# Attention and two gated layers in one kernel: scores merged in PSUM, six low weight halves formed by TensorE and ScalarE, and a new order of steps

## The chip, the cores and the metric

One core of a Trainium2 chip runs the whole program. Its engines are TensorE (PE; its weight loads stand in rows of their own, PEld), VectorE (DVE), ScalarE (ACT), GpSimd (POOL) and SyncE (SP), whose queue issues all DMAs here. The metric is the time of one execution on the device in microseconds, and of several executions the median.

## The reference

Three stages follow one another. Sliding-window attention over 4 batches, 8 heads, 576 positions and head size 64; a feed-forward layer with layer norm on 512 columns and 2048 hidden ones; and a gated layer with GELU, a second layer norm and a product over the sequence.

```python
scores = scale * np.matmul(q, k.transpose(0, 1, 3, 2))
mask = (rel >= 0) & (rel < window)                    # window = 128, rel = row - column
scores = np.where(mask, scores + bias[None], -1e9)    # bias = -slope(head) * |rel|
attn = softmax(scores); x = attn @ v
...
xn = (x - mu) / np.sqrt(var + 1e-06) * g_ln           # x: 4 x 576 x 512
x = x + np.maximum(xn @ w_ch1, 0.0) @ w_ch2           # 512 x 2048, 2048 x 512
...
u, v = split(gelu(x @ w_in))                          # 512 x 1024
v_s = np.einsum('ts,bsd->btd', w_sg, layernorm(v) * g_ln) + b_sg
x = x + (u * v_s) @ w_out
```

The weights come as float64 numbers.

## The kernel before

Phase 1 does attention and the feed-forward layer together, phase 2 the gated layer.

Attention is cut into runs (two query tiles of 128 rows for a pair of heads of a batch; at the end of the sequence a tail) and each run into units, one for each query tile: 72 units, numbered `un`. A query tile of 128 rows sees its own key tile (the columns up to its row) and the previous one (the columns after its row), so that each row needs exactly 128 scores, taken from two tiles. `scores` (L436) writes both tiles' scores of a run into PSUM. `unit` then copies the previous tile's scores to an SBUF tile `t` (L451, ACT or DVE, as the planner chooses; for the first tile of a sequence POOL fills `t` with a large negative number, L467), writes the own tile's scores over it under a mask (L480, `copy_predicated`), adds the distance bias and takes the row's minimum (L486), does the exponentials on ACT (L490), sums and inverts (L493, L494), normalises (L498 on POOL, or L451 on ACT through the same helper), transposes on PE (L508) and writes the two triangles to the tiles `m` (L522 on DVE, or L525 on ACT with L445 on POOL). `values` (L575) multiplies with v, and L555 copies the result to `x`.

The feed-forward layer runs over nine groups `g` of 256 rows. `norm`, `center`, `rest` and `spread` do the layer norm: mean products (L597), `xc` (L610), `xh` (L623), `xl` (L629), squares (L639), their products (L654), the power on POOL (L660) and the spread of rstd (L664). `m1` (L738) and `m2` (L749) are the two products of a step. Every fp32 product is made of three fp32r products of a high and a low half, which is why each operand exists as `h` and `l`. `relu` gives `hh` (L677, ACT) and `hl` (L679, DVE).

Weights are loaded in 40 pieces (`weights(n)`; n below 24 are three quarters of w1 and w2 in pieces of 512 columns; n = 0 to 3 are w1 of the first quarter and 4 to 7 its w2). A piece arrives as float64 and is turned to float32 by the steps of `Split64`: the absolute value of the high word on ACT (L71), and on DVE a clamp (L77), a shift (L79) and two merging steps (L81, L84). Then ACT rounds to the high half (L348), and POOL or DVE subtracts for the low half (L351, "lo"). Phase 2 uses the same steps for its weights (`split64`, L88 and L89 the last two).

The order on every engine's queue is set ahead of time by `Sched`: each task is a generator of `Op`s with an engine, an assumed duration, a priority, the tokens it needs and the buffers it takes. It places, again and again, the ready step with the smallest (start time, priority, number). Constants steer it: HOP and HOPD (time from a step's end to its reader), DVEX (a charge that DVE must undercut where a step could go to another engine), PACE (the priority of units over their number), WFIRST and WBACK (how far ahead of need the weights are put), LQ, OB, OC (offsets in the layer norm, at the transposes and at the values). Unit priorities are the values of PACE; the layer norm of group 0 has start[0] - 14 plus LQ. The first MoE products need the weights 0 to 3 and the four `xl` of group 0, whose input is the values of runs 0 to 3 (units 0 to 7).

```python
# in Split64.bits, the view that steps 0 and 1 (L77, L79) work on, in place
y, yi = (z.rearrange("p (a b) -> p b a", b=2) for z in (x, xi))
# in warm: a product without a reader, when PE has nothing else, until weights piece 23 is done (L790)
yield Op("PE", 110, 10 ** 9)
```

Of the kernel before, what the change touches and what calls it, by code (L numbers as in the profile page):

```python
# [7 lines left out]
F32 = mybir.dt.float32  # L8
F32R = mybir.dt.float32r
U8 = mybir.dt.uint8  # L10
I32 = mybir.dt.int32
ACTF = mybir.ActivationFunctionType
ALU = mybir.AluOpType
# [8 lines left out]
NEG = -1.0e30  # L22
FMAX = float(np.finfo(np.float32).max)
# [11 lines left out]

HOP, HOPD = 160, 127
MOE = 1365
DVEX = 300


PACE = [(0, -61), (7, -47), (8, -46), (15, -32), (16, 4), (23, 12)]
EARLY = 28
WBACK, WFIRST = 5, 40
LBACK = 14, 26
OB, OC = 2, 4
LQ = 0, 1, 2, 3, 4, 8
EPRI = (-1, 9)
# [8 lines left out]
ABANK = 1, 3, 5  # L56


class Split64:


# [11 lines left out]
    def bits(self, k):  # L73
        dve, x, xi = self.nc.vector, self.x, self.x.bitcast(I32)
        y, yi = (z.rearrange("p (a b) -> p b a", b=2) for z in (x, xi))
        if k == 0:
            dve.tensor_scalar(y, y, E_MIN, E_MAX, ALU.max, ALU.min)  # L77
        elif k == 1:
            dve.tensor_scalar(yi, yi, 3, 0x3FFFFFFF, ALU.logical_shift_left, ALU.bitwise_and)  # L79
        elif k == 2:  # L80
            dve.scalar_tensor_tensor(out=xi, in0=self.wh, scalar=-0x40000000, in1=xi, op0=ALU.bitwise_and,  # L81
                                     op1=ALU.bitwise_or)
        else:
            dve.scalar_tensor_tensor(out=xi, in0=self.wl, scalar=29, in1=xi, op0=ALU.logical_shift_right,  # L84
                                     op1=ALU.bitwise_or)
# [28 lines left out]
class Sched:  # L114
# [40 lines left out]
    def run(self, until):  # L155
        while until not in self.done:
            best = None
            for n, p in enumerate(self.procs):
                t = self.ready(p)
# [21 lines left out]
            if op.size:  # L181
                self.dma = max(self.dma, start + 1100) + op.size / 360
                end = self.dma + 1600
            elif op.eng:
                end += HOPD if op.eng == "DVE" else HOP
            if op.token:
# [31 lines left out]
def phase1(tc, nc, a, x2d, cst, p2):  # L218

    sync, act, dve, pool, pe = nc.sync, nc.scalar, nc.vector, nc.gpsimd, nc.tensor  # L220
    ident, ones, g1, mh = cst
    sched = Sched()
# [18 lines left out]
    dist = ap2.tile([128, 12, 128], BF16, name="dist", bufs=1)  # L241
    mask, munf = (ap2.tile([128, 2, 128], U8, name=z, bufs=1) for z in ("mask", "munf"))
    sms = [ap2.tile([128, 8], F32, name="sm%d" % z, bufs=1) for z in range(3)]
# [80 lines left out]
    def weights(n):  # L324
# [12 lines left out]
        j.first()  # L337
        yield Op("DVE", 10 + 1.05 * w, pri)
        j.bits(0)
        yield Op("DVE", 10 + 1.05 * w, pri)  # L340
        j.bits(1)
# [5 lines left out]
        h, l = ((w1 if z < 4 else w2)[q][y][:, z % 4, c] for y in range(2))  # L347
        act.activation(out=h, in_=j.x, func=ACTF.Copy)  # L348
        o = Op(None, 0, pri, token=("w", n), alt=[("POOL", 150 + 2.15 * w, 0), ("DVE", 64 + 1.05 * w, DVEX, 1)])
        yield o  # L350
# [106 lines left out]
    def unit(e):  # L457
# [3 lines left out]
        pri = e.tau  # L461
        sl = [("t", 4, ("T", un))]
        to = [("t", un - 1)] if un else []
        if i == 0:
            yield Op("POOL", 250, pri, need=to, slots=sl, token=("t", un))
            t = ap2.tile([128, 2, 128], F32, tag="t", name="t", bufs=4)
            pool.memset(t, NEG)  # L467
            yield Op(None, 0, pri, need=[("A1", n)])
        else:
            o = Op(None, 0, pri, need=to + [("A1", n)], slots=sl, token=("t", un),  # L470
                   alt=[("ACT", 360), ("DVE", 395, DVEX)] if n in ABANK else [("ACT", 270), ("DVE", 335, DVEX)])
            yield o
            t = ap2.tile([128, 2, 128], F32, tag="t", name="t", bufs=4)
            for h, x in s.parts:
                scaled(o.eng, t[:, h], x[..., u, 0:128])
        w = 64 if tail else 128
        yield Op("DVE", 395 if n in ABANK else 335, pri, need=["msk"], token=("cp", n) if e.last else None)
        for h, x in s.parts:
            k = mask[:, tail, 0:w] if isinstance(h, int) else mask[:, tail:tail + 1, 0:w].to_broadcast([128, 2, w])
            dve.copy_predicated(t[:, h, 0:w], k, x[..., u, 128:128 + w])  # L480
        yield Op("DVE", 425, pri, need=["al2" if tail else "al"], port=True, slots=[("sm", 3, ("nm", un))])
        st = sms[un % 3]
        sums = st[:, 2:6].rearrange("p (h z) -> p h z", h=2)
        for h in range(2):
            d = 8 + s.p + h if tail else 2 * s.p + h
            dve.tensor_tensor_reduce(out=t[:, h], in0=t[:, h], in1=dist[:, d], scale=-0.125, scalar=FMAX, op0=ALU.add,  # L486
                                     op1=ALU.min, accum_out=st[:, h:h + 1])
        yield Op("ACT", 775, pri)
        for h in range(2):
            act.activation(out=t[:, h], in_=t[:, h], func=ACTF.Exp, bias=st[:, h:h + 1], scale=-1.0,  # L490
                           accum_out=sums[:, h, 0:1])
        yield Op("DVE", 160, pri)
        dve.tensor_reduce(out=st[:, 6:8], in_=sums, axis=AX.X, op=ALU.add)  # L493
# [259 lines left out]
    def constants():  # L753
# [6 lines left out]
        sched.free["DVE"] = 2300  # L760
        yield Op("DVE", 200, -1000, need=["cst0"], token="msk")
        dve.tensor_copy(mask, t[:, 3:5])
        yield Op("ACT", 300, -1000, need=["cst0"], token="cst")
        act.activation(out=ident, in_=t[:, 0], func=ACTF.Copy)
        for x0 in range(0, 8, 2):
            yield Op("DVE", 270, -1000, need=["cst0"], token="al" if x0 == 6 else None)
            for x in (x0, x0 + 1):
                dve.tensor_scalar(dist[:, x], t[:, 1], 2.0 ** (2 - x), None, ALU.mult)
# [10 lines left out]
    def warm():  # L779

        z = np_.tile([128, 256], F32, tag="rstd", name="zero", bufs=3).bitcast(BF16)
        dve.memset(z, 0.0)
        ps = ps_a.tile([128, 2, 256], F32, tag="a0", name="warm").rearrange("p a b -> p (a b)")
        for n in range(NWARM):
            pe.matmul(ps, z[:, 0:128], z, start=True, stop=True)
        sched.free["PE"] = 4000
        yield Op(None, 0, 0, need=["al"])
        while ("w", 23) not in sched.done:
            yield Op("PE", 110, 10 ** 9)
            pe.matmul(ob[:, 256:512], dist[:, 0], dist[:, 0:2], start=True, stop=True, skip_group_check=True)  # L790
            yield Op(None, FILL, 10 ** 9)
# [380 lines left out]
def body(tc, nc, a):  # L1172
# [3 lines left out]
    with tc.manual_schedule(), tc.tile_pool(name="cst", bufs=1) as cp:  # L1176
        ident = cp.tile([128, 128], F32, name="ident")
        ones = cp.tile([128, 128], F32, name="ones")
        g1 = cp.tile([128, 4], F32, name="g1")
        mh = cp.tile([128, 1], F32, name="mh")  # L1180
        pool.memset(mh, -0.5)
        pool.memset(ones, 1.0 / DM)
        p2 = Phase2(tc, nc, a, x2d, mh)
        phase1(tc, nc, a, x2d, (ident, ones, g1, mh), p2)

# [47 lines left out]
```

## Time and profile before

| | |
|---|---|
| time, median of 3 runs | 777.67 us (775.90 to 778.61) |
| the profiled execution | 777.32 us, of which the span is 775.2 us |
| PE busy | 749.7 us (97%) |
| DVE busy | 476.5 us (61%) |
| ACT busy | 321.2 us (41%) |
| POOL busy | 217.4 us (28%) |
| mean granted clock of TensorE | 0.976 of full speed |

Matmuls are pipelined, and one of 256 fp32r columns has a row of 0.28 us though the next starts 0.11 us later; so PE counts as busy also where rows only overlap. A row with "x8" joins neighbouring instructions of one kind. Behind a row, square brackets give the idle time of the engine ahead of it and what ended it. On DVE the next instruction often starts some 0.08 us before the row of the last one ends.

### The profile page before, as it was taken

What the parts mean: (1) busy time and instruction counts of PE and PEld (TensorE: products, weight loads), DVE (VectorE), ACT (ScalarE), POOL (GpSimd) and SP (SyncE); (2) the same over time, 40 slices, a digit from 0 to 9 for tenths busy, and PEclk for the clock granted to TensorE, in tenths of its full rate; (3) what the DMA queues carried; (4) which work ended last, traced back from release to release, by engine and by line L of the source; (5) the groups of instructions that cost most, each with busy time, mean ns of one, the idle gap of its engine ahead of it and who ended that gap; (6) DMA issues with size and microseconds to landing.
All of it is one profiled execution on the core that took longest, in us unless ns stands there. A gap on an engine that the chain in (4) does not pass through costs nothing.

```text
span 775.2 us, 15885 instructions
## 1 busy us (share of the span) xinstructions
PE 749.7 (97%) x6258; PEld 693.4 (89%) x6258; DVE 476.5 (61%) x1221; ACT 321.2 (41%) x834; POOL 217.4 (28%) x250
## 2 busy tenths in 40 slices
PE   7779999999999999999999999899899999999998
PEld 3448899999999999999998899899779899999997
DVE  5898999996554543543544445825776645656732
ACT  5777664543442432532423434214354333334410
POOL 1422331121300310301302423208244516416320
PEclk8958999999999999999999999999999999999999
DMA  8562542241112111111111324403240050160002
GB/s 299 145 182 77 174 129 63 77 126 37 49 59 72 34 57 35 43 55 41 43 43 42 83 75 160 135 29 107 79 150 1 28 171 2 47 199 1 1 31 92
DMA packets 51625, 63.41 MB, mean 82 GB/s; under 512 B 10336, under 2 KB 38880, under 8 KB 51552
## 3 DMA queue, kind: packets, MB, share of 16 engines
q1 hardware_dynamic: 51552, 62.41, 25.8%
q8 instruction: 49, 0.80, 0.4%
q14 instruction: 24, 0.20, 0.1%
HBM read 52.96 MB, written 9.44 MB: 80 GB/s over the span
## 4 chain that ended last, share of the span: by engine, by line
PE 84%; DVE 3%; POOL 2%; DMA 1%; issue 1%; ACT 1%; DVEq 0%; POOLq 0%; ACTq 0%
PE ps_h L738 24%; PE acc L749 23%; PE ps_s L1079 8%; PE ps_u L1062 7%; PE ps_o L1107 7%; PE ps_v L986 5%; PE o L575 4%; PE s L436 2%; PE tps L508 2%; DMA st<-in_wo 1%; PE ps_ln L654 1%; POOL x2l L978 1%; PE ps_r L664 1%; DVE sc L84 1%; DVE sc L81 1%
## 5 line engine op out<-in xcount | busy, mean ns | idle before, releaser
L738 PE MATMUL ps_h<-xh,w1h 128*128 128x256 f32 x576 | 166.1, 288 | 1.3 <-DVE hl L679 1.3
L749 PE MATMUL acc<-hh,w2h 128*128 128x256 f32 x576 | 165.6, 287 | 1.4 <-ACT hh L677 1.4
L749 PE MATMUL acc<-hl,w2h 128*128 128x256 f32 x576 | 161.1, 280 | 1.4 <-DVE hl L679 1.4
L738 PE MATMUL ps_h<-xh,w1l 128*128 128x256 f32 x576 | 161.4, 280 | 0.0
L738 PE MATMUL ps_h<-xl,w1h 128*128 128x256 f32 x576 | 161.4, 280 | 0.0
L749 PE MATMUL acc<-hh,w2l 128*128 128x256 f32 x576 | 160.8, 279 | 0.0
L749 PEld LDWEIGHTS acc<-hh,w2h 128*128 128x128 f32 x576 | 109.1, 189 | 6.3 <-issue 2.8
L738 PEld LDWEIGHTS ps_h<-xh,w1h 128*128 128x128 f32 x576 | 109.1, 189 | 3.2 <-issue 1.5
L679 DVE SCALAR_TENSOR_TENSOR hl<-ps_h,hh 128x512 fp32r<-128x512 f32 x72 | 49.6, 690 | 100.5 <-ACT hh L677 100.4
L749 PEld LDWEIGHTS acc<-hl,w2h 128*128 128x128 f32 x576 | 109.1, 189 | 2.0 <-DVE hl L679 1.9
L677 ACT ACTIVATE hh<-ps_h 128x512 fp32r<-128x512 f32 x72 | 42.9, 596 | 161.7 <-PE ps_h L738 161.6
L738 PEld LDWEIGHTS ps_h<-xh,w1l 128*128 128x128 f32 x576 | 109.7, 190 | 0.0
L749 PEld LDWEIGHTS acc<-hh,w2l 128*128 128x128 f32 x576 | 109.4, 190 | 0.0
L738 PEld LDWEIGHTS ps_h<-xl,w1h 128*128 128x128 f32 x576 | 109.1, 189 | 0.0
L498 POOL TENSOR_TENSOR t<-t,sm 128x256 f32<-128x256 f32 x43 | 28.0, 652 | 156.3 <-DVE sm L494 119.2
L490 ACT ACTIVATE t<-t,sm 128x128 f32<-128x128 f32 x144 | 56.2, 392 | 19.6 <-DVE sm L486 19.1
L522 DVE TENSOR_TENSOR m<-tps,munf 128x256 f32<-128x256 f32 x84 | 32.2, 419 | 43.3 <-PE tps L508 43.0
L508 PE MATMUL tps<-ident,t 128*128 128x128 f32 x144 | 30.8, 297 | 10.8 <-POOL t L498 6.2
L71 ACT ACTIVATE sc<-st 128x512 f32<-128x512 f32 (+1 forms) x52 | 30.7, 597 | 18.9 <-DMA st<-in_wo 5.5
L77 DVE TENSOR_SCALAR sc<-sc 128x512 f32<-128x512 f32 (+1 forms) x52 | 29.9, 584 | 13.7 <-ACT sc L71 13.6
L486 DVE CUSTOM_DVE_ANT_0 t<-t,dist 128x128 f32<-128x128 f32 x144 | 38.0, 309 | 0.2
L978 POOL TENSOR_TENSOR gl<-gt,gh 128x576 fp32r<-128x576 f32 x16 | 22.9, 1432 | 53.2 <-ACT gh L977 53.2
(154 smaller groups left out, 1566.7 us busy)
## 6 DMA issues: line engine op xcount, KB each, us to landing
st<-in_w SPq DMA_DIRECT2D x24, 512.0 KB, 4.4
x2d<-x SPq DMA_DIRECT2D x18, 256.0 KB, 2.0
out<-xr SPq DMA_DIRECT2D x15, 288.0 KB, 2.1
st<-in_w SPq DMA_DIRECT2D x16, 256.0 KB, 2.9
st<-in_wi SPq DMA_DIRECT2D x8, 512.0 KB, 4.1
st<-x2d SPq DMA_DIRECT2D x8, 512.0 KB, 5.4
xr<-x2d SPq DMA_DIRECT2D x8, 512.0 KB, 6.4
rq<-in_q SPq DMA_DIRECT2D x28, 128.0 KB, 2.8
```

Source lines behind the costliest of these rows:

```text
L486: dve.tensor_tensor_reduce(out=t[:, h], in0=t[:, h], in1=dist[:, d], scale=-0.125, scalar=FMAX, op0=ALU.add, op1=ALU.min, accum_out=st[:, ...
L490: act.activation(out=t[:, h], in_=t[:, h], func=ACTF.Exp, bias=st[:, h:h + 1], scale=-1.0, accum_out=sums[:, h, 0:1])
L508: pe.transpose(tp[:, h], t[:, h], ident)
L522: dve.tensor_tensor(out=out, in0=tp[0:k], op=ALU.mult, in1=munf[0:k, y:y + 1].to_broadcast([k, 2, 128]))
L677: act.activation(out=h, in_=ps, func=ACTF.Relu)
L679: dve.scalar_tensor_tensor(out=l, in0=ps, scalar=0.0, in1=h.bitcast(F32), op0=ALU.max, op1=ALU.subtract)
L738: pe.matmul(ps[:, half], w[:, kc, f], m[:, kc], start=kc == 0 and x == 0, stop=kc == 3 and x == 2)
L749: pe.matmul(accs[half][:, d], w[:, f, ds], m[:, k], start=fi and d == 0 and k == 0 and x == 0, stop=la and k == 1 and x == 2, skip_group_c ...
L986: self.nc.tensor.matmul(ps, xs[s][:, kc, c0:c0 + 128], self.wv[m][:, kc], start=kc == 0 and x == 0, stop=kc == 3 and x == 2)
L1062: pe.matmul(ps[:, z, 0:288], wu[s][:, kc, ds], self.x[m][:, kc, 288 * z:288 * z + 288], start=kc == 0 and x == 0, stop=kc == 3 and x == 2)
L1079: pe.matmul(ps[:, z, 0:288], l, r[:, 288 * z:288 * z + 288], start=n == 0, stop=n == len(mm) - 1)
L1107: pe.matmul(ps[:, z, 0:288], wo[s][:, kc, ds], gated[b][m][:, kc, 288 * z:288 * z + 288], start=n == 0, stop=n == 11)
```

## The change

The previous tile's scores are no longer copied out. The own tile's scores are merged under the mask into the previous tile's place in PSUM (for a first tile, a column `far` of large negative numbers is merged into the own tile's place under a third, inverted mask), and the distance step reads PSUM and writes `t`. The score bank is given back after the distance step instead of after the masked copy. For the weights 0 to 5 the low half is formed by two products, identity times x and minus identity times the high half, accumulated in a bank of `ps_h`, and a copy by ACT. L77 and L79 work on the contiguous tile. The planner's constants change, its assumed durations for the changed steps too, and `warm` issues two small products at a time.

```diff
-HOP, HOPD = 160, 127
+HOP, HOPD, HOPP = 160, 127, 280
-DVEX = 300
-PACE = [(0, -61), (7, -47), (8, -46), (15, -32), (16, 4), (23, 12)]
+DVEX = 600
+PACE = [(0, -64), (7, -59), (8, -46), (15, -32), (16, 4), (23, 12)]
-WBACK, WFIRST = 5, 40
+WBACK, WFIRST = 9, 36
-OB, OC = 2, 4
-LQ = 0, 1, 2, 3, 4, 8
+OB, OC = 3, 0
+LQ = 1, 0, 3, 2, 4, 8
+NLO = 6
...
-        y, yi = (z.rearrange("p (a b) -> p b a", b=2) for z in (x, xi))
-            dve.tensor_scalar(y, y, E_MIN, E_MAX, ALU.max, ALU.min)
+            dve.tensor_scalar(x, x, E_MIN, E_MAX, ALU.max, ALU.min)
-            dve.tensor_scalar(yi, yi, 3, 0x3FFFFFFF, ALU.logical_shift_left, ALU.bitwise_and)
+            dve.tensor_scalar(xi, xi, 3, 0x3FFFFFFF, ALU.logical_shift_left, ALU.bitwise_and)
...
-                self.dma = max(self.dma, start + 1100) + op.size / 360
+                self.dma = max(self.dma, start + 1100) + op.size / 300
-                end += HOPD if op.eng == "DVE" else HOP
+                end += {"DVE": HOPD, "PE": HOPP}.get(op.eng, HOP)
...
-        yield Op("DVE", 10 + 1.05 * w, pri)
+        yield Op("DVE", 75 + .51 * w, pri, port=True)
         j.bits(0)
-        yield Op("DVE", 10 + 1.05 * w, pri)
+        yield Op("DVE", 75 + .51 * w, pri, port=True)
         j.bits(1)
...
         act.activation(out=h, in_=j.x, func=ACTF.Copy)
+        if n < NLO:
+            yield Op("PE", 1080, pri, need=["cst"], slots=[("h", 2, ("w", n))])
+            ps = ps_h.tile([128, 2, 256], F32, tag="h", name="ps_w").rearrange("p a b -> p (a b)")
+            pe.matmul(ps, ident, j.x, start=True, stop=False)
+            pe.matmul(ps, minus, h, start=False, stop=True)
+            yield Op("ACT", 490, pri, token=("w", n))
+            act.activation(out=l, in_=ps, func=ACTF.Copy)
+            return
...
-        sl = [("t", 4, ("T", un))]
-        to = [("t", un - 1)] if un else []
-        if i == 0:
-            yield Op("POOL", 250, pri, need=to, slots=sl, token=("t", un))
-            t = ap2.tile([128, 2, 128], F32, tag="t", name="t", bufs=4)
-            pool.memset(t, NEG)
-            yield Op(None, 0, pri, need=[("A1", n)])
-        else:
-            o = Op(None, 0, pri, need=to + [("A1", n)], slots=sl, token=("t", un),
-                   alt=[("ACT", 360), ("DVE", 395, DVEX)] if n in ABANK else [("ACT", 270), ("DVE", 335, DVEX)])
-            yield o
-            t = ap2.tile([128, 2, 128], F32, tag="t", name="t", bufs=4)
-            for h, x in s.parts:
-                scaled(o.eng, t[:, h], x[..., u, 0:128])
-        yield Op("DVE", 395 if n in ABANK else 335, pri, need=["msk"], token=("cp", n) if e.last else None)
+        yield Op("DVE", 395 if n in ABANK else 335, pri, need=["msk", ("A1", n)])
         for h, x in s.parts:
-            k = mask[:, tail, 0:w] if isinstance(h, int) else mask[:, tail:tail + 1, 0:w].to_broadcast([128, 2, w])
-            dve.copy_predicated(t[:, h, 0:w], k, x[..., u, 128:128 + w])
-        yield Op("DVE", 425, pri, need=["al2" if tail else "al"], port=True, slots=[("sm", 3, ("nm", un))])
+            m = tail if i else 2
+            k = mask[:, m, 0:w] if isinstance(h, int) else mask[:, m:m + 1, 0:w].to_broadcast([128, 2, w])
+            if i:
+                dve.copy_predicated(x[..., u, 0:w], k, x[..., u, 128:128 + w])
+            else:
+                dve.copy_predicated(x[..., u, 128:256], k, far.to_broadcast([128, 128]) if isinstance(h, int)
+                                    else far.rearrange("p (o c) -> p o c", o=1).to_broadcast([128, 2, 128]))
+        yield Op("DVE", 425, pri, need=["al2" if tail else "al"] + ([("t", un - 1)] if un else []),
+                 slots=[("sm", 3, ("nm", un)), ("t", 4, ("T", un))], token=("t", un))
+        t = ap2.tile([128, 2, 128], F32, tag="t", name="t", bufs=4)
...
-            dve.tensor_tensor_reduce(out=t[:, h], in0=t[:, h], in1=dist[:, d], scale=-0.125, scalar=FMAX, op0=ALU.add,
+            f = slice(0, 128) if i else slice(128, 256)
+            dve.tensor_tensor_reduce(out=t[:, h], in0=s.S[h][:, u, f], in1=dist[:, d], scale=-0.125, scalar=FMAX, op0=ALU.add,
                                      op1=ALU.min, accum_out=st[:, h:h + 1])
+        if e.last:
+            sched.done["cp", n] = sched.free["DVE"] + HOPD
-        yield Op("DVE", 160, pri)
+        yield Op("DVE", 260, pri)
...
+        dve.tensor_scalar(mask[:, 2], t[:, 3], -1.0, 1.0, ALU.mult, ALU.add)
+        act.activation(out=minus, in_=t[:, 0], func=ACTF.Copy, scale=-1.0)
...
-            yield Op("PE", 110, 10 ** 9)
-            pe.matmul(ob[:, 256:512], dist[:, 0], dist[:, 0:2], start=True, stop=True, skip_group_check=True)
+            yield Op("PE", 213, 10 ** 9)
+            for x in range(2):
+                pe.matmul(ob[:, 256:512], dist[:, 0], dist[:, 0:2], start=True, stop=True, skip_group_check=True)
```

## Rows read from the trace of the kernel before

**Rows 1.** Windows: us, busy of PE, PEld, DVE, ACT, POOL; granted clock; DMA

```profile
10.00:65.00 55.00, 43.47 (x311) 26.01 (x312) 46.01 (x171) 39.34 (x134) 18.11 (x30) 0.72 0.62 195
65.00:112.00 47.00, 47.00 (x421) 43.50 (x420) 45.02 (x127) 33.14 (x93) 14.78 (x18) 1.00 0.46 139
112.00:470.00 358.00, 358.00 (x3354) 337.45 (x3353) 198.75 (x632) 142.21 (x429) 69.10 (x101) 1.00 0.20 57
470.00:500.00 30.00, 27.43 (x229) 26.82 (x229) 25.92 (x39) 12.25 (x24) 10.95 (x9) 0.94 0.43 150
```

**Rows 2.** Chain of work that ended last: start, us, what; up to the first products

```profile
61.23 1.15 PE ps_r L664 x4
...
63.68 1.73 PE ps_ln L597 x8
65.52 5.69 PE ps_h L738 x48
```

**Rows 3.** Timeline of DVE, 63.7 to 65.6 us

```profile
63.75 1.27 DVE L629 SCALAR_TENSOR_TENSOR xl<-xc,g,xh 128x256 fp32r<-128x256 f32 x3
64.94 0.68 DVE L351 TENSOR_TENSOR w2l<-sc,w2h 128x512 fp32r<-128x512 f32 x1
65.54 0.68 DVE L610 TENSOR_TENSOR xc<-x,ps_ln 128x512 f32<-128x512 f32 x1
```

**Rows 4.** Line 351 up to 65 us, DVE

```profile
L351 DVE TENSOR_TENSOR w2l<-sc,w2h x3: 683/684/692, 52.1 to 64.9; 128x512 fp32r<-128x512 f32 x3
L351 DVE TENSOR_TENSOR w1l<-sc,w1h x2: 674/677/680, 33.3 to 40.8; 128x512 fp32r<-128x512 f32 x2
```

**Rows 5.** Timeline of DVE, split steps alone and beside POOL

```profile
17.51 0.42 DVE L77 TENSOR_SCALAR sc<-sc 128x512 f32<-128x512 f32 x1
17.84 0.28 DVE L486 CUSTOM_DVE_ANT_0 t<-t,dist 128x128 f32<-128x128 f32 x1
...
43.80 1.49 DVE L79 TENSOR_SCALAR sc<-sc 128x512 int32<-128x512 int32 x1
```

**Rows 6.** Timeline of POOL at 43.6 us

```profile
43.56 1.44 POOL L351 TENSOR_TENSOR w1l<-sc,w1h 128x512 fp32r<-128x512 f32 x1
```

**Rows 7.** Windows with line 77 alone, then with line 79 alone

```profile
10.00:65.00 55.00, 5.41 (x10) 0.72 0.62 195
...
10.00:65.00 55.00, 5.24 (x8) 0.72 0.62 195
```

**Rows 8.** Groups by line and form, 0 to 180 us

```profile
L81 DVE SCALAR_TENSOR_TENSOR sc<-st,sc 128x512 int32<-128x512 int32 x24 | 16.3, 688 | 0.0
...
L679 DVE SCALAR_TENSOR_TENSOR hl<-ps_h,hh 128x512 fp32r<-128x512 f32 x17 | 11.7, 685 | 1.7 <-ACT hh L677 1.6
...
L677 ACT ACTIVATE hh<-ps_h 128x512 fp32r<-128x512 f32 x17 | 10.1, 595 | 8.5 <-PE ps_h L738 8.4
```

**Rows 9.** Waits of DVE, 10 to 65 us: us in total, times, longest

```profile
DVE w2l L351 <- ACT w2h L348: 1.6, 1, 1.6
DVE t L480 <- ACT t L451: 1.4, 2, 0.9
```

**Rows 10.** Timeline of PE, small layer-norm products twice

```profile
53.04 3.57 PE L654 MATMUL ps_ln<-ones,sq 128*128 128x1 f32 x16 [0.64 <-ACT sq L639]
...
71.05 1.84 PE L654 MATMUL ps_ln<-ones,sq 128*128 128x1 f32 x16
```

**Rows 11.** Groups by line and form, 0 to 65 us

```profile
L451 ACT ACTIVATE t<-s 128x256 f32<-128x256 f32 x9 | 3.2, 376 | 7.1 <-PE s L436 4.8 <-DVE t L480 1.6 <-ACT xh L623 0.8
...
L453 DVE COPY t<-sa 128x128 f32<-128x128 f32 x2 | 0.5, 287 | 1.7 <-PE sa L436 1.7
L453 DVE COPY t<-s 128x256 f32<-128x256 f32 x1 | 0.4, 425 | 0.1
```

**Rows 12.** Timeline of all engines around 93 us

```profile
92.34 0.68 DVE L351 TENSOR_TENSOR w1l<-sc,w1h 128x512 fp32r<-128x512 f32 x1
...
93.34 0.36 PE L738 MATMUL ps_h<-xh,w1h 128*128 128x256 f32 x1
```

More of the change, by code (lines that the diff above doesn't have):

```diff
@@ L220, in phase1 @@
     sync, act, dve, pool, pe = nc.sync, nc.scalar, nc.vector, nc.gpsimd, nc.tensor
-    ident, ones, g1, mh = cst
+    ident, minus, ones, g1, mh, far = cst
     sched = Sched()
@@ L241, in phase1 @@
     dist = ap2.tile([128, 12, 128], BF16, name="dist", bufs=1)
-    mask, munf = (ap2.tile([128, 2, 128], U8, name=z, bufs=1) for z in ("mask", "munf"))
+    mask, munf = (ap2.tile([128, n, 128], U8, name=z, bufs=1) for n, z in ((3, "mask"), (2, "munf")))
     sms = [ap2.tile([128, 8], F32, name="sm%d" % z, bufs=1) for z in range(3)]
@@ L760, in constants @@
         sched.free["DVE"] = 2300
-        yield Op("DVE", 200, -1000, need=["cst0"], token="msk")
-        dve.tensor_copy(mask, t[:, 3:5])
-        yield Op("ACT", 300, -1000, need=["cst0"], token="cst")
+        yield Op("DVE", 320, -1000, need=["cst0"], token="msk")
+        dve.tensor_copy(mask[:, 0:2], t[:, 3:5])
+        dve.tensor_scalar(mask[:, 2], t[:, 3], -1.0, 1.0, ALU.mult, ALU.add)
+        yield Op("ACT", 550, -1000, need=["cst0"], token="cst")
         act.activation(out=ident, in_=t[:, 0], func=ACTF.Copy)
+        act.activation(out=minus, in_=t[:, 0], func=ACTF.Copy, scale=-1.0)
         for x0 in range(0, 8, 2):
@@ L1177, in body @@
         ident = cp.tile([128, 128], F32, name="ident")
+        minus = cp.tile([128, 128], F32R, name="minus")
         ones = cp.tile([128, 128], F32, name="ones")
         g1 = cp.tile([128, 4], F32, name="g1")
-        mh = cp.tile([128, 1], F32, name="mh")
+        mh = cp.tile([128, 2], F32, name="mh")
+        mh, far = mh[:, 0:1], mh[:, 1:2]
         pool.memset(mh, -0.5)
+        pool.memset(far, NEG)
         pool.memset(ones, 1.0 / DM)
         p2 = Phase2(tc, nc, a, x2d, mh)
-        phase1(tc, nc, a, x2d, (ident, ones, g1, mh), p2)
+        phase1(tc, nc, a, x2d, (ident, minus, ones, g1, mh, far), p2)
 def wsT(w):
```

## The prediction

> **What bounds the kernel now.** I read the busy time by stretch first. From 65 us to 470 us TensorE (PE) is busy in every microsecond at the full clock, whatever VectorE (DVE) does: DVE is at 45.0 of 47 us up to 112 us and at 198.8 of 358 after it [rows 1]. [...] So two things set the time: when the first MoE product starts, and whether anything later opens a hole in PE. The products after the start are the same in both kernels.
>
> Next the chain up to the first MoE product, at 65.5 us. Its last links are PE pieces one behind the other (rstd of group 0, the mean of group 1) [rows 2], but the operand is no earlier: the last three `xl` of group 0 run on DVE from 63.75 to 65.0 us [rows 3]. They come so late because the planner gives steps that are ready at once to DVE by priority, and the layer norm's (start minus 14) comes behind units 0 to 15 (PACE up to -32) and weights 0 to 7 (need minus 40, now 36). That order stays: PACE, WFIRST and LQ move the numbers, not their ranking. So I price the change by the DVE work and the DVE waits that leave the head.
>
> **The parts.** *lo of weights 0 to 5.* Five lo's ran on DVE before 65 us [rows 4]; the other three of the first eight on POOL (one of them in [rows 6]); of the six concerned four were on DVE. One holds DVE 0.60 us from its start to the next start (64.94 to 65.54) [rows 3]: 4 x 0.60 = **-2.4 us**. In return PE gets an fp32 product of 512 columns and an fp32r one. [...] ACT gets six copies from PSUM at 0.60 [rows 8], 3.6 us, against nine score copies of 3.2 us that leave it [rows 11]: even.
>
> *Scores merged in PSUM.* The copies of the previous tile's scores go. On DVE that is 0.5 + 0.4 us in the head [rows 11], less what overlaps, **-0.8 us**. The memsets on POOL go as well; POOL is no bound. DVE also waited 1.4 us for the copies and 1.6 us for the `h` of a lo [rows 9]; both waits go, but what comes next on DVE may be late too (scores, transposes), so I take half, **-1.5 us**, between 0 and -3.0. The distance step now reads PSUM. No row has it so. The two-source steps `hl` (from PSUM, 685 ns) and L81 (from SBUF, 688 ns) cost the same [rows 8]; the one-source copy of 256 elements from PSUM took 0.42 us [rows 11], as much as 512 elements in SBUF [rows 5], so half the speed. The step has two sources, so I take 0; the far end, 32 steps at twice 0.29 us, is +9.3. The same holds for the masked copy, which read PSUM already and now writes it too: no row, 0. The score bank is held until after the distance step instead of after the masked copy, but no longer waits for ACT: 0.
>
> [...]
>
> *Split steps contiguous.* The old form visits even elements and then odd ones. L77 nevertheless runs 0.42 us, 0.33 start to start, with POOL silent (17.51 to 17.84) [rows 5]: 512 elements at that rate leave contiguous order nothing to win. What lengthens these steps is POOL: L79 at 43.80 took 1.49 us while POOL's subtraction ran from 43.56 to 45.00 [rows 5, 6]. The 18 steps between 10 and 65 us took 5.41 + 5.24 us [rows 7], 3.1 over 18 x 0.42. Two of POOL's subtractions and the memsets leave; the rest of POOL's work stays, and DVEX 600 sends more to it. I take half, **-1.5 us** (0 to -3.1).
>
> [...]
>
> *More small products.* Late in the head PE is slow: the same 16 small LN products took 3.57 us at 53 us and 1.84 at 71 us [rows 10]. A steadier clock would shorten the last links of the chain, but `xl` on DVE holds the start to 0.5 us before it [rows 2, 3]: **-0.3 us**, between 0 and -1.7 (that pair of rows).
>
> *Order set anew.* HOPP, the DMA rate 300, DVEX, PACE and OB/OC change only which step is put first. DVE idles 55 - 46.0 = 9.0 us between 10 and 65 us [rows 1], 3.0 of it counted above [rows 9]. The other 6.0 can be won; as much can be lost if a step is put in front of a late one. I take 0, ends -6 and +6. The loads' SP order moves with this; no load ends a link of the chain shown.
>
> **Sum.** -2.4 - 0.8 - 1.5 - 1.5 - 0.3 = -6.5 us on DVE's way to the first product, which then starts near 59 us. Behind it PE must stay fed: the last lo of the next quarter's four weights ran from 92.34 us, and the product that I take to need it started at 93.34 [rows 12]. That is tight, but DVE's queue is unbroken (45.0 of 47) [rows 1], so it moves with the start. I leave 0.5 us there: -6.0. The profiled execution took 777.32 us (span 775.2), so 771.3; it lies 0.35 under the median of the three runs (777.67), so **771.7 us** to be measured.
>
> **Rivals.** *Slower: PE's queue in the head.* [...] Chance 0.14 (with a distance step that is slow from PSUM, which gives the same sign).
>
> *No gain: the feed.* PE starts 6 us earlier and waits at the second quarter's weights, because DVE's work between 65 and 112 us is not less (45.0 of 47) [rows 1]; 0.5 to 1 us is left: 776.7 to 777.2. For it: the tight row at 93 us [rows 12]. Against it: the savings lie ahead of that work on the same queue. Chance 0.16.
>
> *Contiguous order does win*, if the 3.1 us of excess were the stride and not POOL: all of it goes, 1.6 more than I count: 770.1. Chance 0.05.
>
> *The order wins more*: some 5 of the 6 us of other idle time: 766.7. The hole at 470 to 500 us, where PE is busy 27.4 of 30 us and DVE 25.9 [rows 1], could close with a new order as well, up to 2.6. Chance 0.15.
>
> **Chances and range.** My case 0.50, within 767.5 to 774.5 (the waits, the collisions and the clock between their ends). Faster by over 0.3% (2.3 us, about what this measurement can tell): 0.50 + 0.05 + 0.15 = 0.70; within it 0.16; slower 0.14. The range goes from 765.5 (below the better order, with part of its hole) to 778.5 (past the feed, short of PE's queue in full), leaving about 0.1 at each end.
>
> **What would show it.** Right: first MoE product between 57 and 61 us; DVE's L351 rows before it down from five to one or two; L77 and L79 alone still 0.42 us; distance steps still 0.29 us; PE full from the start to 470 us. Wrong: contiguous steps under 0.40 us (third rival); distance steps over 0.35 us; PE waiting for ACT's `h` or for lo's copies before the first product (first rival); PE holes of 1 us and more at 85 to 110 us (second); a first product before 55 us (fourth). A hole after 470 us that is larger by 3 us or more would spoil the sum though each step held.

## The result, and the profile after

The kernel after takes **765.48 us** (median of four runs, 765.15 to 765.54); the kernel before, run beside it on the same chip, 778.14. The ratio is 0.9837, interval 0.9808 to 0.9865. The forecast was 771.7 with a range from 765.5: the direction was right, the gain of 12.7 us is twice the 6.0 of the sum, and the time lies just below the range's lower end. The profiled execution took 765.15 us, of which the span is 763.4.

Windows of the kernel after (columns as in [rows 1]):

```profile
10.00:65.00 55.00, 50.27 (x433) 35.94 (x434) 49.16 (x194) 49.12 (x164) 21.98 (x39) 0.97 0.65 214
65.00:112.00 47.00, 47.00 (x424) 43.78 (x422) 42.59 (x109) 28.25 (x74) 17.51 (x23) 1.00 0.48 138
112.00:470.00 358.00, 358.00 (x3349) 336.78 (x3348) 171.47 (x540) 130.72 (x396) 104.30 (x167) 1.00 0.20 59
470.00:500.00 30.00, 27.71 (x228) 27.51 (x228) 24.80 (x39) 11.25 (x21) 9.02 (x7) 0.94 0.38 117
```

Against [rows 1], PE is again full from 65 to 470 us. What changed lies before: in the head, ACT is now at 49.1 of 55 us for 39.3, and the granted clock is 0.97 for 0.72.

Chain of work that ended last, 50 to 54 us:

```profile
49.83 0.70 PE s L444 x12
50.54 0.03 issue
50.56 1.99 PE ps_ln L602 x8
52.56 1.54 PE ps_h L743 x13
```

Timeline of DVE, 47 to 50.7 us:

```profile
46.88 0.42 DVE L77 TENSOR_SCALAR sc<-sc 128x512 f32<-128x512 f32 x1
47.22 0.48 DVE L634 SCALAR_TENSOR_TENSOR xl<-xc,g,xh 128x256 fp32r<-128x256 f32 x1
47.62 0.42 DVE L79 TENSOR_SCALAR sc<-sc 128x512 int32<-128x512 int32 x1
47.95 0.48 DVE L634 SCALAR_TENSOR_TENSOR xl<-xc,g,xh 128x256 fp32r<-128x256 f32 x1
...
49.80 0.83 DVE L634 SCALAR_TENSOR_TENSOR xl<-xc,g,xh 128x256 fp32r<-128x256 f32 x1
```

The first MoE product's row starts at 52.21 us, where before it was 65.27 (the chains of both kernels show it some 0.3 us later [rows 2]). The last `xl` of group 0 ends near 50.6, 1.6 us ahead of that start, where before it ended at 65.02 [rows 3], 0.25 us ahead: DVE no longer ends the head alone. Product 1200 of `m1` starts at 391.4 us for 404.0, so 12.5 of the 13.1 us are still there; at the end of the span it is 11.8 (763.4 for 775.2), so the rest of the kernel adds nothing.

Groups by line and form, 10 to 52.2 us, on DVE:

```profile
L489 DVE CUSTOM_DVE_ANT_0 t<-s,dist 128x128 f32<-128x128 f32 x23 | 5.5, 286 | 0.2
...
L77 DVE TENSOR_SCALAR sc<-sc 128x512 f32<-128x512 f32 x7 | 3.4, 481 | 0.0
L79 DVE TENSOR_SCALAR sc<-sc 128x512 int32<-128x512 int32 x7 | 3.1, 441 | 0.1
```

Timeline of PE, one of the new low halves and what follows it:

```profile
48.59 1.02 PE L352 MATMUL ps_w<-sc,ident 128*128 128x512 f32 x2
49.04 0.79 PE L353 MATMUL ps_w<-w2h,minus 128*128 128x512 f32 x1
49.76 0.77 PE L444 MATMUL s<-rk,rq 64*64 64x64 f32 x16
```

From the pair's start to the next product's it is 1.17 us; the other five took 1.09 to 1.20, where [rows 2] give 1.10 (half of 1.73 for the fp32 product, twice 5.69/48 for the other; an estimate). ACT's copy of it, by line, 10 to 52.2 us:

```profile
L355 ACT ACTIVATE w1l<-ps_w 128x512 fp32r<-128x512 f32 x4 | 2.3, 585 | 0.0
```

### The profile page after: what moved, and what is told of

The parts are those of the page before. It is cut to its first block, busy times and chain, and to the rows that moved or that the text cites. A ratio compares the mean times of both kernels' runs of the same rounds, so it can differ in the third digit from the quotient of the medians.

```text
span 763.4 us, 15899 instructions
## 1 busy us (share of the span) xinstructions
PE 746.2 (98%) x6270; PEld 692.8 (91%) x6270; DVE 444.7 (58%) x1129; ACT 311.7 (41%) x805; POOL 256.6 (34%) x327
## 4 chain that ended last, share of the span: by engine, by line
PE 90%; POOL 3%; DMA 2%; ACT 2%; DVE 2%; issue 1%; SPq 0%; DVEq 0%; POOLq 0%; ACTq 0%
PE acc L754 25%; PE ps_h L743 24%; PE ps_s L1087 8%; PE ps_u L1070 7%; PE ps_o L1115 7%; PE ps_v L994 6%; PE o L580 4%; PE s L444 3%; PE tps L513 2%; PE ps_ln L659 1%; DMA st<-in_wo 1%; PE ps_ln L602 1%; DMA st<-in_w 1%; POOL x2l L986 1%; PE ps_w L352 1%
## 5 line engine op out<-in xcount | busy, mean ns | idle before, releaser
L453 POOL TENSOR_SCALAR_AFFINE_SELECT m<-m 128x256 f32<-128x256 f32 x118 | 53.1, 452 | 154.5 <-ACT m L530 151.2
L503 POOL TENSOR_TENSOR t<-t,sm 128x256 f32<-128x256 f32 x52 | 32.9, 634 | 90.0 <-DVE sm L499 70.5
L530 ACT ACTIVATE m<-tps 128x256 f32<-128x256 f32 x62 | 23.7, 382 | 85.2 <-PE tps L513 84.8
L1028 ACT ACTIVATE ge<-ge 128x512 f32<-128x512 f32 (+1 forms) x34 | 22.4, 658 | 37.1 <-DVE ge L1027 37.1
L81 DVE SCALAR_TENSOR_TENSOR sc<-st,sc 128x512 int32<-128x512 int32 (+1 forms) x52 | 36.0, 696 | 0.4
```

What stands on the lines that cost most here:

```text
L453: pool.affine_select(out=out, in_=in_, pattern=pat, compare_op=ALU.is_ge, fill=0.0, base=-1 if up else 0, channel_multiplier=1 if up else -1)
L503: pool.tensor_tensor(out=t, in0=t, op=ALU.mult, in1=st[:, 6:8].rearrange("p (h o) -> p h o", o=1).to_broadcast([128, 2, 128]))
```

## The experiments

Theories in the order in which they were held. At first three sources were in question for the 6 us that the sum lacked: the changed instructions, the new order, and the clock that the small products hold up (**C**); the first expectations say what each would give. Then, the order being left, **X, Y, Z**: one group of the planner's numbers is the cause (DVEX; the assumed costs; the ranks). **M**: the numbers move the triangle steps (the masked copy of the transposed weights from PSUM to `m`, L522 before, L527 after) from DVE to ACT and POOL. **F, J**: the gain belongs to one particular order that any move loses, or to all the numbers jointly.

All kernels, each timed beside the kernel before on its chip (whose median there lay between 776.25 and 778.14 us, so that differences of 1 us between rows say little; the ratios allow for it). The first products and counts are of one profiled execution each. "First product" is the start of the first `m1` row; "triangles" are DVE's triangle instructions from 10 us up to it (a first tile's unit needs one, the others two).

| kernel | median us (lowest to highest) | ratio to before, 95% | first product | triangles |
|---|---|---|---|---|
| after | 765.48 (765.15 to 765.54) | 0.9837 (0.9808 to 0.9865) | 52.2 | 3 |
| after, old plan | 771.25 (767.50 to 775.88) | 0.9926 (0.9898 to 0.9954) | 58.0 | 14 |
| before, new plan | 776.29 (773.22 to 778.82) | 0.9998 (0.9975 to 1.0020) | 57.5 | 6 |
| after, one small product | 766.20 (764.28 to 768.30) | 0.9870 (0.9840 to 0.9900) | 54.0 | 3 |
| before, two small products | 776.65 (772.25 to 779.57) | 0.9997 (0.9973 to 1.0020) | 64.2 | 14 |
| after, strided split | 764.81 (763.95 to 765.78) | 0.9848 (0.9823 to 0.9874) | 52.2 | 3 |
| after, lo as before | 772.23 (770.37 to 773.58) | 0.9943 (0.9921 to 0.9965) | 53.9 | 5 |
| after, scores copied | 771.16 (769.94 to 771.80) | 0.9928 (0.9902 to 0.9954) | 54.9 | 11 |
| before, merged scores | 771.69 (770.24 to 775.90) | 0.9945 (0.9922 to 0.9968) | 60.4 | 16 |
| after, DVEX 300 | 771.24 (770.91 to 773.42) | 0.9932 (0.9908 to 0.9955) | 57.5 | 14 |
| after, old plan, DVEX 600 | 770.47 (768.84 to 775.01) | 0.9929 (0.9901 to 0.9957) | 57.9 | 11 |
| after, old costs | 773.63 (771.09 to 776.70) | 0.9960 (0.9942 to 0.9979) | 59.3 | 9 |
| after, old ranks | 768.32 (766.20 to 772.88) | 0.9896 (0.9867 to 0.9926) | 59.7 | 12 |
| after, triangles to DVE | 772.38 (770.09 to 772.96) | 0.9930 (0.9911 to 0.9950) | 58.6 | 14 |
| after, old plan, triangles to ACT | 771.85 (768.97 to 774.50) | 0.9928 (0.9904 to 0.9952) | 59.0 | 11 |
| after, handover 300 | 766.57 (766.36 to 769.75) | 0.9867 (0.9846 to 0.9888) | 54.3 | 3 |
| after, DVEX 560 | 765.72 (765.08 to 767.89) | 0.9853 (0.9831 to 0.9875) | 55.2 | 12 |
| after, old plan, triangles as after | 765.67 (765.36 to 768.87) | 0.9859 (0.9836 to 0.9881) | 54.5 | 3 |
| after, triangles as old plan | 772.18 (771.22 to 773.33) | 0.9933 (0.9915 to 0.9952) | 55.9 | 14 |

### Code against plan

The planner's numbers of one kernel put into the other: constants, and the assumed costs of steps that both have.

```diff
-HOP, HOPD, HOPP = 160, 127, 280
+HOP, HOPD = 160, 127
-DVEX = 600
+DVEX = 300
-PACE = [(0, -64), (7, -59), (8, -46), (15, -32), (16, 4), (23, 12)]
+PACE = [(0, -61), (7, -47), (8, -46), (15, -32), (16, 4), (23, 12)]
-WBACK, WFIRST = 9, 36
+WBACK, WFIRST = 5, 40
-OB, OC = 3, 0
-LQ = 1, 0, 3, 2, 4, 8
+OB, OC = 2, 4
+LQ = 0, 1, 2, 3, 4, 8
...
-        yield Op("DVE", 75 + .51 * w, pri, port=True)
+        yield Op("DVE", 10 + 1.05 * w, pri)
...
```

> The kernel after with the planner's numbers of before: all changed instructions stay, the order is set with the old costs and constants. Theory P: 770 to 776 us, first product 4 to 9 us later than 52.2. Theory C: 765 to 768 us. Theory D (prediction's sum, 6 us, from VectorE's work alone): 770 to 773 us.

> The kernel before with the planner's numbers of after alone (HOPP, DVEX, PACE, WBACK, WFIRST, OB, OC, LQ, the DMA rate, the assumed costs of L77, L79 and the sums); no instruction is changed, only the order. Theory P: 768 to 773 us, first product 4 to 9 us earlier. Theory C, and D: 775.5 to 780 us.

The changed instructions under the old plan are the prediction: first product at 58.0 us ("near 59"), 771.25 us (771.7), though its ten executions spread from 767.50 to 775.88. The plan in the old code gives nothing that can be measured, where theory P had 768 to 773. Its first product does come at 57.5, but PE then waits for the layer norm of the groups (waits of PE, 55 to 112 us):

```profile
PE ps_h L738 <- DVE xl L629: 3.6, 2, 2.1
```

Of the 7.8 us of lead 1.7 are left at product 168. So the two halves of the gain, 5.9 us (from 777.15 of the kernel before beside it) and 5.8, are not two independent sums: the plan's half needs the code's.

### The parts of the code

Small products, back to one and, in the kernel before, up to two:

```diff
-            for x in range(2):
+            for x in range(1):
                 pe.matmul(ob[:, 256:512], dist[:, 0], dist[:, 0:2], start=True, stop=True, skip_group_check=True)
```

> The kernel after, with one small product at each filling place instead of two; the order of everything else is the same. [...] Theory P (the planner's new costs and constants do it) and theory D (VectorE's saved work alone, as in the prediction's sum): 765 to 766.5 us, first product within 1 us of 52.2.

> The kernel before with two small products at each filling place, order otherwise as before. Theory C: clock in the head from 0.72 to above 0.9, first product 3 to 6 us earlier than 65.3, 771 to 775 us. Theories P and D: 776.5 to 779 us.

In time both are within what can be told from no change. Neither moved the clock as far as C had it (below 0.85 and a first product 3 to 6 us later with one, above 0.9 with two): with one small product the granted clock from 10 to 52 us is 0.92 for 0.96 and the first product comes 1.8 us later; with two in the kernel before it is 0.81 for 0.72 in the head, and the first product comes 1.1 us earlier. The sharper test is one stretch. Windows of the kernel before with two small products:

```profile
40.00:50.00 10.00, 6.20 (x50) 3.85 (x48) 9.93 (x28) 6.35 (x20) 4.38 (x7) 0.76 0.52 164
50.00:60.00 10.00, 8.48 (x60) 5.76 (x60) 6.97 (x26) 7.83 (x23) 2.06 (x5) 0.73 0.66 177
```

The same windows of the kernel before:

```profile
40.00:50.00 10.00, 6.66 (x50) 3.40 (x44) 9.93 (x27) 6.43 (x20) 4.38 (x7) 0.67 0.57 192
50.00:60.00 10.00, 8.04 (x40) 5.54 (x40) 6.75 (x26) 7.80 (x23) 2.06 (x5) 0.50 0.65 183
```

From 50 to 60 us the granted clock rises from 0.50 to 0.73 and DVE does what it did: PE's clock was not what ended the head. Theory C falls as the cause of 6 us; 1 to 2 us at the first product remain possible.

The stride of L77 and L79, put back into the kernel after with its order unchanged:

```diff
+        y, yi = (z.rearrange("p (a b) -> p b a", b=2) for z in (x, xi))
-            dve.tensor_scalar(x, x, E_MIN, E_MAX, ALU.max, ALU.min)
+            dve.tensor_scalar(y, y, E_MIN, E_MAX, ALU.max, ALU.min)
...
-            dve.tensor_scalar(xi, xi, 3, 0x3FFFFFFF, ALU.logical_shift_left, ALU.bitwise_and)
+            dve.tensor_scalar(yi, yi, 3, 0x3FFFFFFF, ALU.logical_shift_left, ALU.bitwise_and)
```

> The kernel after with the old visiting order (even elements, then odd) in L77 and L79; the planner's costs, and so the order of all instructions, stay those of after. If contiguous order itself is nothing (the prediction's value): 765 to 766.5 us, L77 alone 0.42 us, first product within 1 us of 52.2. If it is a gain in itself (the third rival): 767 us and more, L77 and L79 longer in total by 1.6 us or more before the first product.

Groups of that kernel, 10 to 52.2 us:

```profile
L77 DVE TENSOR_SCALAR sc<-sc 128x512 f32<-128x512 f32 x7 | 3.1, 449 | 0.0
L79 DVE TENSOR_SCALAR sc<-sc 128x512 int32<-128x512 int32 x7 | 3.0, 421 | 0.1
```

449 and 421 ns strided against 481 and 441 contiguous: the contiguous order is worth nothing.

Low halves as before, by POOL and DVE:

```diff
-NLO = 6
+NLO = 0
```

> The kernel after with NLO = 0: the first six low halves are formed by VectorE or GpSimd again, planned with the new numbers. Theory D (work saved on VectorE counts one for one, 2.4 us and part of the waits): 768 to 770 us, first product 2.4 to 4 us later than 52.2. Rival: these products matter little, since GpSimd takes the low halves at DVEX 600: 765 to 767 us.

Timeline of PE in that kernel, around the first products:

```profile
53.90 0.36 PE L743 MATMUL ps_h<-xh,w1h 128*128 128x256 f32 x1
56.55 0.39 PE L743 MATMUL ps_h<-xl,w1h 128*128 128x256 f32 x1 [2.29 <-DVE xl L634]
...
58.75 0.58 PE L743 MATMUL ps_h<-xl,w1h 128*128 128x256 f32 x1 [1.58 <-DVE xl L634]
```

The first product comes early, but the four `xl` of its group run only at 56.02 us and, three in a row, from 58.22: low halves stand around them on DVE, at 52.60, 53.54, 57.02 and 59.41, 0.69 us each. That is the queue that the prediction's first term emptied. The loss, 6.8 us, is larger than either theory had it, and most of it (3.9 us of PE's waits) comes after the first product.

The merge, undone in the kernel after (`unit` of before) and done alone in the kernel before:

```diff
...
+            for h, x in s.parts:
+                scaled(o.eng, t[:, h], x[..., u, 0:128])
...
-                dve.copy_predicated(x[..., u, 0:w], k, x[..., u, 128:128 + w])
+            dve.copy_predicated(t[:, h, 0:w], k, x[..., u, 128:128 + w])
...
-            dve.tensor_tensor_reduce(out=t[:, h], in0=s.S[h][:, u, f], in1=dist[:, d], scale=-0.125, scalar=FMAX, op0=ALU.add,
+            dve.tensor_tensor_reduce(out=t[:, h], in0=t[:, h], in1=dist[:, d], scale=-0.125, scalar=FMAX, op0=ALU.add,
...
```

> The kernel after with the unit of before (previous tile's scores copied to SBUF by ScalarE or VectorE, own scores merged there, distance step from SBUF, the fill on GpSimd), planned with the new numbers. Theory D (0.8 us of VectorE and half the waits on ScalarE): 767 to 769 us. Rival M (the merge is the main part: ScalarE and VectorE are both full in the head, and a copy stands in every unit's chain): 770 to 774 us, first product 4 us or more later.

> The kernel before with the scores merged in PSUM alone; planner's numbers, low halves and split steps as before. Theory D: 774 to 776 us. Rival M: 770 to 773 us. If the distance step is slower from PSUM, its rows take over 0.35 us.

Alone it brings almost what the whole code does under the old plan: the low halves (with the split steps and the small products) then add 2.4 us at the first product (60.4 to 58.0) but 0.4 to the time. Without it the kernel after loses 5.7, as rival M of these two runs had it, though its first product is only 2.7 us later and not 4. Undoing it also sends triangles back to DVE (11 for 3), with ACT taking score copies again; so the undone parts (5.7, 6.8 and 5.8 for merge, low halves and plan) add up to 18, not to 12.7. Waits of DVE in the kernel before with merged scores, 10 to 62 us:

```profile
DVE m L518 <- PE tps L504: 1.0, 4, 0.3
DVE s L470 <- PE s L436: 0.7, 2, 0.5
```

These two lines are all: the waits of [rows 9] are gone and nothing as long took their place. In this kernel DVE is busy for 47.9 of the 50.4 us up to its first product.

### The numbers of the plan, one group at a time

In the first kernel only DVEX goes back (the diff below); in the second everything goes back but DVEX; in the third the assumed costs alone (PE's handover, the DMA rate, the splits, the reduce); in the fourth the ranks alone (PACE, WBACK, WFIRST, OB, OC, LQ).

```diff
-DVEX = 600
+DVEX = 300
```

> The kernel after with DVEX at 300 again, nothing else. Theory X (DVEX is the term that the prediction took at 0: at 600 the planner hands some 15 triangle steps (scores times 1/sum) from DVE to ACT and POOL, 0.34 us each of DVE before 112 us): back to what the kernel after took with the whole old plan, 770 to 772, with some 18 of these steps on DVE up to 112 us and a first product near 58 us. Rival Y (the planner's costs: the splits at their contiguous price, PE's handover 280, the reduce 260): 765 to 766.5. Rival Z (the ranks PACE, WFIRST, WBACK, OB, OC, LQ): 765 to 766.5.

> The kernel after with all old numbers of the planner but DVEX, which stays 600. Theory X: DVEX alone brings what the new plan brought, 765 to 767, with some 4 triangle steps on DVE up to 112 us. Rivals Y and Z: no gain over the whole old plan, 770 to 772.

> [...] Theory X and rival Z: 765 to 766.5. Rival Y: 770 to 772.

> The kernel after with the old ranks alone (PACE, WBACK, WFIRST, OB, OC, LQ); DVEX and the costs are those of after. Theory X and rival Y: 765 to 766.5. Rival Z: 770 to 772.

(The first of these texts calls the triangle steps "scores times 1/sum"; the steps that it means are the masked copies.) Each of the three groups undone loses time (5.8, 8.2, 2.8 us), and DVEX alone on the old plan brings 0.8, within the spread. X, Y and Z fall, each as the only cause. What the four have in common stands in the last column: nine to fourteen triangles on DVE, not three. The count does not rank them, though: nine went with 773.63 us, twelve with 768.32.

### The triangle steps

The engine of a triangle step is chosen by price, `("ACT", 275, 740)` against `("DVE", 670 or 335, DVEX)`: assumed duration plus charge, counted from the time at which that engine could start. First the price of ACT was moved by 300 ns each way (up in the kernel after, down to 440 in the same kernel with the old plan), and beside it two numbers of the kernel after by 7%, for theory F: HOPP from 280 to 300, and DVEX from 600 to 560.

```diff
-               need=[("bl", un - 1)] if un else [], alt=[("ACT", 275, 740)] + ([] if tail else [("DVE", 670 if i else 335, DVEX)]))
+               need=[("bl", un - 1)] if un else [], alt=[("ACT", 275, 1040)] + ([] if tail else [("DVE", 670 if i else 335, DVEX)]))
```

> The kernel after with one price: the triangle step (mask of the transposed weights out of PSUM) is 300 ns dearer on ACT, 1040 for 740, so that the planner puts most of them on DVE again. Theory M (what the order won is triangle steps that leave a full DVE): the first product comes 4 to 7 us later than 52.2 and the time is 769 to 772. Theory F (the last 6 us belong to one particular order, and any other loses them whatever it moves): the same time, but then the two small moves sent with it lose 3 us and more as well. If DVE has room, 765 to 767.

> The kernel after with the whole old plan, and in it the triangle step 300 ns cheaper on ACT, 440 for 740, so that most leave DVE for ACT and POOL as they do in the kernel after. Theory M: most of the missing 6 us, 765 to 768, with a first product at 52 to 55 us. Theory F: 769 to 773, as with the whole old plan (771.25).

> The kernel after with one number moved by 7%: PE's handover 300 for 280 in the planner. It changes the order in places and moves hardly any work between engines. Theory M: within 1.5 us of 765.5. Theory F: 768 to 772, and a first product 3 us and more later.

> The kernel after with DVEX at 560 for 600. Some 25 steps of the whole kernel go to DVE again. Theory M: within 2 us of 765.5, as most triangle steps stay off DVE before 52 us. Theory F: 768 to 772, and a first product 3 us and more later.

F falls: small moves of a number leave 766.57 and 765.72, though the first products came 2.1 and 3.0 us later. Of M's two runs one came out as forecast but for 0.4 us, 772.38; the other missed, but it tested little, since 11 of the 14 triangles stayed on DVE. DVEX 560 speaks against M: twelve on DVE and 765.72.

So the last two runs fixed the engine of the triangle steps of units 0 to 23 and nothing else: with the old plan, ONDVE holds the units that the kernel after gave to DVE (0, 4, 6, 22); in the kernel after, those of the old plan (0, 1, 2, 4, 6, 9, 10, 12, 13, 16, 20, 22, 23).

```diff
-               need=[("bl", un - 1)] if un else [], alt=[("ACT", 275, 740)] + ([] if tail else [("DVE", 670 if i else 335, DVEX)]))
+               need=[("bl", un - 1)] if un else [], alt=([("DVE", 670 if i else 335, 0)] if un in ONDVE else [("ACT", 275, 0)]) if un < 24 else [("ACT", 275, 740)] + ([] if tail else [("DVE", 670 if i else 335, DVEX)]))
```

> The kernel after with the whole old plan (771.25), and in it the engine of each triangle step of units 0 to 23 fixed as the kernel after chose it: four of 24 on DVE (0, 4, 6, 22) for thirteen. Theory M (these steps, 11 fewer on DVE before the first product, are the 6 us): first product at 53 to 55 us, 766 to 768. Theory J (the order's numbers work jointly: triangle steps, splits and layer norm all have to leave DVE ahead of the first product): the freed time is taken by other steps, first product at 56 us or later, 769 to 772.

> The kernel after, with the engine of each triangle step of units 0 to 23 fixed as the old plan chose it: thirteen of 24 on DVE for four. Theory M: first product at 56 to 58 us, 769 to 771.5. Theory J: part of it, a first product at 53 to 56 us and 765.5 to 768.5, as with DVEX at 560, where twelve of them ran on DVE before 52 us and the time was 765.72.

765.67 and 772.18: in time, moving nine units' steps makes up the whole difference between the plans, in both directions, and neither interval meets that of the kernel it started from (0.9859 for 0.9926, 0.9933 for 0.9837). The times lie 0.3 and 0.7 us outside M's ranges and over 3 us outside J's, though the second first product (55.9) is one that J allowed. M stands for the time; that the other new numbers bring nothing beyond it holds only for the sum, as shown below. The rows of line 527 (with its ACT and POOL counterparts, 530 and 453), from 10 us to the first product. The kernel before:

```profile
L522 DVE TENSOR_TENSOR m<-tps,munf 128x256 f32<-128x256 f32 x14 | 5.4, 418 | 2.3 <-PE tps L508 2.1
```

The kernel after:

```profile
L527 DVE TENSOR_TENSOR m<-tps,munf 128x256 f32<-128x256 f32 x3 | 1.3, 425 | 1.1 <-PE tps L513 0.8 <-ACT m L530 0.3
...
L530 ACT ACTIVATE m<-tps 128x256 f32<-128x256 f32 x13 | 5.0, 381 | 2.6 <-PE tps L513 2.5
...
L453 POOL TENSOR_SCALAR_AFFINE_SELECT m<-m 128x256 f32<-128x256 f32 x25 | 11.6, 470 | 13.4 <-ACT m L530 12.8
```

The kernel after with the old plan, and then the same with the triangles as after:

```profile
L527 DVE TENSOR_TENSOR m<-tps,munf 128x256 f32<-128x256 f32 x14 | 5.5, 419 | 2.3 <-PE tps L513 2.2
```

```profile
L527 DVE TENSOR_TENSOR m<-tps,munf 128x256 f32<-128x256 f32 x3 | 1.3, 419 | 0.3 <-ACT t L495 0.3
...
L453 POOL TENSOR_SCALAR_AFFINE_SELECT m<-m 128x256 f32<-128x256 f32 x25 | 12.7, 510 | 8.4 <-ACT m L530 7.5
```

Eleven instructions of 0.42 us, 4.2 us of DVE, become six copies of 0.38 us on ACT and eleven selects of 0.5 us on POOL, which had room. Windows up to the first product, the three kernels of this family: old plan, old plan with the triangles as after, and after.

```profile
10.00:58.03 48.03, 40.85 (x346) 25.11 (x347) 43.78 (x182) 39.51 (x134) 14.06 (x27) 0.96 0.69 232
```

```profile
10.00:54.50 44.50, 38.13 (x311) 23.94 (x311) 40.05 (x170) 40.13 (x138) 21.45 (x38) 0.92 0.76 246
```

```profile
10.00:52.20 42.20, 37.47 (x324) 23.17 (x325) 37.51 (x164) 38.18 (x135) 20.15 (x38) 0.96 0.73 240
```

The fixed triangles take 3.7 us of work off DVE (43.78 to 40.05) and the first product comes 3.5 us earlier; idle DVE stays at 4.2 to 4.5 us. At product 1200 the lead over the old plan is 4.1 us, and by the end of the span 5.0 (768.6 to 763.6): some 0.9 us of the difference is made after product 1200, which was not followed further.

The way back is less clean. In the kernel after with the triangles as the old plan (first product at 55.88 us, 3.7 later than in the kernel after):

```profile
10.00:55.88 45.88, 39.88 (x335) 24.83 (x335) 39.16 (x167) 38.11 (x132) 14.63 (x25) 0.93 0.68 219
```

DVE's work grows by only 1.6 us (37.51 to 39.16), since it has got less far with other steps, and its idle time by 2.0 (4.7 to 6.7). Of the 5.8 us by which the span is longer, 3.7 stand at the first product and 1.9 more at product 168.

The other new numbers do win something, and lose it again. The kernel after is 2.3 us ahead of the old plan with the triangles as after at the first product, 3.8 at product 1200 (391.4 us for 395.3), and 0.2 at the end of the span. Products 1200 to 1500 take 93.3 us in the first and 90.2 in the second. This goes with the ranks: it is 90.0 to 90.3 us in all six kernels with merged scores and the old ranks, and 91.8 to 94.6 in all kernels with the new ones. In the kernel after, PE waits there once (2.3 us, at 478 us), and its granted clock from 470 to 500 us is 0.94. The wait, and the window of 470 to 500 us in the old plan with the triangles as after:

```profile
PE ps_ln L659 <- POOL sq L651: 2.3, 1, 2.3
```

```profile
470.00:500.00 30.00, 28.89 (x253) 28.71 (x252) 20.23 (x32) 8.35 (x15) 7.36 (x6) 1.00 0.34 112
```

So the close agreement of 765.67 with 765.48 is in part luck: the triangles are 4.1 of the 7.9 us that the new plan has won by product 1200, and of the other 3.8 that the rest of the new numbers has won nearly all is given back. The old ranks show the same: 6.7 us behind the kernel after at product 1200 (398.1 us), 3.3 at the end of the span (766.7).

Some things stay open. With DVEX 560 the head is 2.7 us worse than in the kernel after (product 1200 at 394.2 us for 391.4), as M has it, and the profiled execution is 2.7 us longer, 767.89 us; but its other three runs took 765.08 to 766.23, so M's price was not confirmed there. Why twelve triangles on DVE cost next to nothing there and the fourteen of the fixed engines 6.7 us is not shown. Nor did a run take apart which of the ranks opens the wait at 478 us.

## Why the prediction was right on the code and wrong on the order

**What bounds the kernel** was right in naming two things, the first MoE product and holes in PE after it; in the kernel after PE stays full from that product to 470 us. The first product alone does not tell the time: the seven kernels that have it between 53.9 and 55.9 us took from 765.67 to 772.23 us, and the old ranks, at 59.7, took 768.32. That `xl` on DVE ends the head was right for before; after, PE's chain to the first product shows no such wait.

**The failed step is "Order set anew"**, taken at 0 with ends of -6 and +6; it measured -5.8 us (771.25 to 765.48), almost its far end. Its first sentence says that HOPP, DVEX, PACE and the others "change only which step is put first". They also choose the engine: with DVEX at 600 a two-part triangle step costs DVE 670 + 600 against ACT's 275 + 740, where with 300 DVE was cheaper (970 to 1015). That moved 4.2 us of work off the engine whose way to the first product the prediction itself priced, by a row of the kernel before that could have been priced (L522, 14 instructions, 5.4 us). With those engines fixed and every other number old, the time was 765.67. The collision term noticed that DVEX "sends more" to POOL and did not ask what that takes off DVE. The fourth rival named the right size (766.7) from the wrong source, DVE's idle time: between the plans idle time hardly moves (4.2 to 4.7 us), work does (43.8 to 37.5). Nor did the hole at 470 to 500 us close, which that rival also named: PE is busy 27.7 of 30 us there for 27.4; in the old plan with the triangles as after it is 28.9.

**The rest of the sum held**: -6.5 to the first product forecast, -7.2 measured under the old plan (65.27 to 58.03). Its terms held less well, so that the sum agrees in part by luck. DVE's work ahead of the first product fell by 2.5 us (46.3 up to 65.27 us, to 43.8) where lo, copies and collisions were to give 4.7, partly because more units are done by then (34 distance steps for 28); DVE's idle time fell by 4.7 (9.0 to 4.2) where the waits were to give 1.5. Of merge and low halves the merge is the larger, not the smaller: alone it brings the first product 4.9 us forward, to 60.4, and idle DVE to 2.5 us, against its 2.3 of terms.

**Lo on TensorE** has no cost for PE in the sum: right, with the pair (1.09 to 1.20 us) near the 1.10 of [rows 2] and ACT's copy (0.59) as forecast. What PE's queue would cost, on which the chance of 0.14 and the top of the range lean, was the author's estimate and is shown by no run; from 10 us to the first product of the kernel after PE is busy 37.5 of 42.2 us at a granted clock of 0.96. The first rival would have shown PE waiting for ACT's `h`. Waits of PE in the kernel after, 10 to 112 us, the longest two:

```profile
PE tps L513 <- POOL t L503: 3.9, 2, 3.1
PE tps L513 <- POOL m L453: 0.8, 1, 0.8
```

None is a lo product. The second line is a wait for one of the moved triangles. On DVE no lo is left before the first product; under the old plan it is two, and one or two were forecast.

**Distance step from PSUM** at 0: right, 286 ns in 23 steps against 0.28 us from SBUF [rows 5].

**Contiguous split** at 0: right, by the strided run, with 449 and 421 ns strided for 481 and 441 contiguous. **Collisions** with POOL: L77 and L79 took 6.5 us for 14 steps, 0.6 over 14 x 0.42, where before the excess was 3.1 over 18 [rows 7]; so 2.5 of it is gone for the 1.5 that was counted, though POOL is busier than before.

**The clock** at -0.3, with up to -1.7: the runs that change the small products moved the first product by 1.1 and 1.8 us and the time by 0.5 and 0.7, which is not clear of the spread. **The feed**: the second rival's place, 85 to 110 us, shows no hole in the kernel after. A hole of its kind, with `xl` in place of the weights, is in the kernel before with the new plan, where 3.6 us of waits for `xl` came with the loss of the lead.

**After 470 us** PE waits about as long as before. Waits of PE in the kernel after, 500 to 600 us:

```profile
PE acc L754 <- ACT hh L682: 2.0, 1, 2.0
PE ps_v L994 <- DVE vg L1031: 1.3, 1, 1.3
PE acc L754 <- DVE hl L684: 0.5, 1, 0.5
```

## What to carry to other kernels

Where a planner picks the engine of a step by price, a change of its constants is a change of work, not of order: list the steps that have a second engine, price each on the engine that bounds the stretch, and take that sum as the far end. An engine's way to a deadline is its work ahead of it plus its idle time; reading both windows to the same event tells which of the two a change has moved. A lead at one event is not yet time won: read it again at later ones, where another part of the same change can give it back. And undoing one part of a planned kernel moves other steps too: fix their engines before the difference is called the part's.

## What the runs showed of the hardware

The length of DVE's split steps did not go with how much POOL works. L77 and L79 averaged 0.59 us in the kernel before [rows 7], where POOL is busy 18.1 of 55 us [rows 1], three of its instructions there being subtractions like the one of 1.44 us beside which a split step took 1.49 [rows 5, 6]. In the kernel after, with one such subtraction and POOL busy 20.2 of 42 us, largely with 25 selects of 0.47 us, they averaged 0.46. No run isolated it.
